# Retention attention in front of a GELU MLP: 64-token sub-chunks on four 64x64 TensorE tiles, and a new emission order

## The chip, the cores and the metric

The kernel runs on one core of a Trainium2 chip. A core has TensorE (PE, the matmul engine; its weight loads are listed apart as PEld), VectorE (DVE), ScalarE (ACT), GpSimd (POOL) and SyncE (SP), each with its own queue that it works off in order, and 16 DMA engines that all queues share. Matmuls write to PSUM, eight banks of 512 fp32 columns in each of 128 partitions; everything else lives in SBUF. The metric is the device time of one execution in microseconds.

## The reference

A retention layer (attention without softmax, with a decay per head) feeds an MLP with the exact GELU. Batch 8, 8 heads, 576 tokens, 64 per head; so 4608 tokens of 512, and 2048 hidden units.

```python
scale = 1.0 / np.sqrt(D_)
scores = scale * np.matmul(q, k.transpose(0, 1, 3, 2))
gamma = 1.0 - 2.0 ** (-5.0 - np.arange(H))
rel = pos[:, None] - pos[None, :]
Dmat = np.where(rel >= 0, gamma[:, None, None] ** rel[None, :, :], 0.0)
ret = np.matmul(scores * Dmat[None], v)          # per batch and head
x = ret.transpose(0, 2, 1, 3).reshape(B * S, H * D)
h = x @ w_in
out = (0.5 * h * (1.0 + erf(h / np.sqrt(2)))) @ w_out
```

Inputs and output are fp32; both kernels compute in bf16 with fp32 sums.

## The kernel before

**Attention in chunks.** Each sequence of 576 tokens is cut into four chunks of 128 and one of 64: 40 chunks, numbered through the batch. The decay between two tokens splits into a factor for the row and one for the column, so v is scaled once (`vh`, L242, table `dv`), the scores get only a causal mask (L235), and the output gets its factor when it leaves PSUM (L288, table `dq`). What came before a chunk enters through a running sum of k times v per head, which is kept in a PSUM bank for a whole sequence (`u_ps`, L266) and copied to SBUF by ACT after each chunk (`u_sb`, L270).

For one chunk TensorE does: transposes of q and k (`turn`, L213; 8 matmuls with an identity), which DVE or ACT copies to `qkT`; `scores` (L226: 8 matmuls, per pair of heads one on rows 0 to 63 and one on rows 64 to 127 of the array); `inner` (L260: 8 matmuls, masked scores times `vh`; L266: 4 for the running sum); and `cross` (L280: 8 matmuls, q times the running sum, on two halves of the rows). `evacuate` (L288) then writes x with tokens on partitions. The MLP wants x with features on partitions, so x is transposed once more: for chunks 0 to 8 on TensorE (`turn_x`, L302, copied at L303), from chunk 9 on by a DMA transpose from SP (L294). From chunk 9 on q and k are transposed by DMA too (L207).

**The MLP in blocks.** Nine blocks of 512 tokens. Product 1 (`mlp1_step`, L314) makes 16 tiles of 128 hidden units, four matmuls each, and ACT applies GELU (L318). Product 2 (`mlp2_step`, L343) sums 16 matmuls for each of four groups of 128 tokens; ACT copies the result (L349) and SP stores it (L350). The last group of all goes in three column pieces (L331, L334, L335).

**Order.** The scheduler is off; the kernel writes every engine's order itself. A planner keeps an estimated clock (`now`), a list of attention steps that are due (T transposes, R scores with the cross of the chunk before, S inner, U a late cross, V the scaled v, X the transpose of x), and hands out MLP steps where no attention step is due. RR takes two chunks in one visit. `LEAD`, `PAIR_LEAD` and `LATE_LEAD` limit how far attention runs ahead. Blocks 0 and 1 are cut into pieces of tokens (0 to 256, 256 to 512; 0 to 192, 192 to 320 or 448, and the rest mixed between the steps of product 2).

**PSUM.** Five banks (a to e) are shared by scores, transposes, hT and oT; two hold `o_ps`, one `u_ps`.

**Loads.** Chunk 0 comes as fp32 by three DMAs from SP (L84), which DVE casts (L132, L133). All other chunks (L137) and both weights (L149, L159; 8 pieces each) come from POOL's queue, which casts to bf16 on the way: chunks 1 to 3, w_in, chunk 4, four pieces of w_out, chunk 5, three, chunk 6, the last; then one chunk after each S.

The two lines that set how scores are spread over the array:

```python
sl = slice(64 * e, 64 * e + 64)                                    # L225
nc.tensor.matmul(sc[e][:cs, hp, :cs], lhsT=qkT[sl, 1, hp, :cs], rhs=qkT[sl, 0, hp, :cs], ...)   # L226
```

Of the kernel before, what the change touches and what calls it, by code (L numbers as in the profile page):

```python
# [13 lines left out]
ALU = mybir.AluOpType  # L14


@with_exitstack
def kernel(
# [9 lines left out]

# [8 lines left out]

    HP = H // 2
    C = 128
# [4 lines left out]
    NCH = -(-S // C)  # L48
    chunks = [(b, ci, ci * C, min(C, S - ci * C)) for b in range(B) for ci in range(NCH)]
    N_CH = len(chunks)  # L50
    N_PE_TR = 9
    N_FIRST = 4
    N_LD = 7
    LEAD = 52
    PAIR_FROM = 2
    PAIR_LEAD = 70
    LATE_LEAD = 48
# [4 lines left out]
    tr_pool = ctx.enter_context(tc.tile_pool(name="tr", bufs=9))  # L62
    ret_pool = ctx.enter_context(tc.tile_pool(name="ret", bufs=2))
    v_pool = ctx.enter_context(tc.tile_pool(name="v", bufs=5))
    x_pool = ctx.enter_context(tc.tile_pool(name="x", bufs=4))
    u_pool = ctx.enter_context(tc.tile_pool(name="u", bufs=4))
    g_pool = ctx.enter_context(tc.tile_pool(name="g", bufs=2))
    o_pool = ctx.enter_context(tc.tile_pool(name="o", bufs=4))

    PS = bass.MemoryType.PSUM  # L70

    ps = ctx.enter_context(tc.tile_pool(name="ps", bufs=1, space=PS))

    xT = const_pool.tile([128, N_DM, n_tok], BF16, name="xT")


    zeros = const_pool.tile([128, 512], BF16, name="zeros")
    nc.vector.memset(zeros, 0.0)

    clock = [0.0]  # L80
    first = []
    for nm, src in (("q32", q), ("k32", k), ("v32", v)):
        t = const_pool.tile([128, H, D], FP32, name=nm)
        nc.sync.dma_start(t, src[0, :, 0:C, :].rearrange("h s d -> s h d"))  # L84
        first.append(t)
    ident = const_pool.tile([128, 128], BF16, name="ident")
    make_identity(nc, ident)

    lg_row = const_pool.tile([128, H, 1], FP32, name="lg_row")
    for h in range(H):  # L90
        nc.vector.memset(lg_row[:, h], log_gamma[h])
    ln_scale = const_pool.tile([128, 1], FP32, name="ln_scale")
    nc.vector.memset(ln_scale, math.log(scale))
    msk = const_pool.tile([128, 1, 128], FP32, name="msk")
    nc.vector.memset(msk, 1.0)

    pos = const_pool.tile([128, 1, NCH], FP32, name="pos")
    nc.gpsimd.iota(pos[:, 0, :], pattern=[[C, NCH]], base=0, channel_multiplier=1,
                   allow_small_or_imprecise_dtypes=True)

    nc.gpsimd.affine_select(
        out=msk[:, 0, :], in_=msk[:, 0, :], compare_op=ALU.is_ge, fill=0.0, base=0,
        pattern=[[1, 128]], channel_multiplier=-1,
    )

    arg = const_pool.tile([128, H, NCH], FP32, name="arg")
    nc.vector.tensor_tensor(arg, lg_row.to_broadcast([128, H, NCH]), pos.to_broadcast([128, H, NCH]), op=ALU.mult)
    dv = const_pool.tile([128, H, NCH], FP32, name="dv")
    nc.scalar.activation(dv, arg, AF.Exp, scale=-1.0, bias=ln_scale)
    dq = const_pool.tile([128, H, NCH], FP32, name="dq")  # L110
    nc.scalar.activation(dq, arg, AF.Exp)

    warm_act = const_pool.tile([128, 1], FP32, name="warm_act")
    nc.scalar.activation(warm_act, ln_scale, AF.Gelu)


    ret_short = [const_pool.tile([128, HP, 128], BF16, name=f"ret_short{e}") for e in range(2)]
    vh_short = const_pool.tile([128, H, D], BF16, name="vh_short")
    for t in ret_short + [vh_short]:
        nc.gpsimd.memset(t, 0.0)  # L120


    loaded = {}
    land_chunk, land_in, land_out = {}, [], []
    dma_clock = [2.0]

    def load_chunk(i, now=0.0):
        b, ci, c0, cs = chunks[i]
        qk = ld_pool.tile([128, 2, H, D], BF16, tag="qk", name="qk_ld")
        if i == 0:  # L130
            v_ld = first[2]
            nc.vector.tensor_copy(qk[:, 0], first[0])  # L132
            nc.vector.tensor_copy(qk[:, 1], first[1])  # L133
        else:
            v_ld = ld_pool.tile([128, H, D], BF16, tag="v", name="v_ld")
            for dst, src in ((qk[:, 0], q), (qk[:, 1], k), (v_ld, v)):
                nc.gpsimd.dma_start(dst[:cs], src[b, :, c0:c0 + cs, :].rearrange("h s d -> s h d"))  # L137
        loaded[i] = (qk, v_ld)
        dma_clock[0] = max(dma_clock[0], now) + 3.0 * cs / C
        v_at = 6.5 if i == 0 else dma_clock[0] + (1.2 if i < N_FIRST else 1.6)  # L140
        land_chunk[i] = (v_at - 1.9, v_at - 0.9, v_at)

    W_IN_COLS = 256
    w_in_sb, w_out_sb = [], []

    def load_w_in():
        j = len(w_in_sb)
        t = const_pool.tile([128, N_DM, W_IN_COLS], BF16, name=f"w_in{j}")
        nc.gpsimd.dma_start(  # L149
            t, moe_w_in[:, j * W_IN_COLS:(j + 1) * W_IN_COLS].rearrange("(c p) f -> p c f", p=128)  # L150
        )
        w_in_sb.append(t)
        dma_clock[0] += 1.38
        land_in.append(dma_clock[0] + (1.9 if j else 1.3))

    def load_w_out():
        j = len(w_out_sb)
        t = const_pool.tile([128, 2, d_model], BF16, name=f"w_out{j}")
        nc.gpsimd.dma_start(  # L159
            t, moe_w_out[j * 256:(j + 1) * 256, :].rearrange("(c p) f -> p c f", p=128)  # L160
        )
        w_out_sb.append(t)
        dma_clock[0] += 1.38
        land_out.append(dma_clock[0] + 1.3)

    for i in range(4):
        load_chunk(i)
    for _ in range(d_ff // W_IN_COLS):
        load_w_in()
    load_chunk(4)  # L170
    for j in range(N_DF // 2):
        load_w_out()
        if j in (3, 6):
            load_chunk(5 + (j == 6))
    


    st = {i: {} for i in range(N_CH)}
    u_ps = [None]
    mlp_begun = [False]  # L180

    free_at = dict.fromkeys("abcde", 0.0)
    held = set()
    last_tag = [None]

    def first_free(n=1):
        return sorted((x for x in free_at if x not in held), key=lambda x: free_at[x])[:n]

    def bank(until, shape, dtype, name):

        tag = last_tag[0] = first_free()[0]
        free_at[tag] = clock[0] + until
        return ps.tile(shape, dtype, tag=tag, name=name)

    def tr_ps(shape, name):

        return bank(1.3, shape, BF16, name)

    def turn(i, parts=(0, 1)):

        cs = chunks[i][3]
        qk = loaded[i][0]
        if "qkT" not in st[i]:
            st[i]["qkT"] = tr_pool.tile([128, 2, HP, 128], BF16, tag="qkT", name="qkT")
        qkT = st[i]["qkT"]
        if i >= N_PE_TR:
            nc.sync.dma_start(qkT.rearrange("p j hp s -> p (j hp) s")[:, :, :cs],  # L207
                              qk[:cs].rearrange("p j h d -> p (j h d)"), transpose=True)
            return
        for j in parts:  # L210
            ps = tr_ps([128, HP, 128], "qk_ps")
            for hp in range(HP):
                nc.tensor.transpose(ps[:, hp, :cs], qk[:cs, j, 2 * hp:2 * hp + 2, :], ident[:cs, :cs])  # L213
            if i >= N_FIRST:
                nc.vector.tensor_copy(qkT[:, j, :, :cs], ps[:, :, :cs])  # L215
            else:
                nc.scalar.copy(qkT[:, j, :, :cs], ps[:, :, :cs])

    def scores(i, banks):
        cs = chunks[i][3]  # L220
        qkT = st[i]["qkT"]
        sc = [ps.tile([128, HP, 128], FP32, tag=banks[e], name=f"sc{e}") for e in range(2)]
        for hp in range(HP):
            for e in range(2):
                sl = slice(64 * e, 64 * e + 64)  # L225
                nc.tensor.matmul(sc[e][:cs, hp, :cs], lhsT=qkT[sl, 1, hp, :cs], rhs=qkT[sl, 0, hp, :cs],  # L226
                                 start=True, stop=True)
        return sc

    def masked(i, sc):  # L230
        b, ci, c0, cs = chunks[i]
        st[i]["ret"] = []
        for e in range(2):
            r = ret_short[e] if cs < C else ret_pool.tile([128, HP, 128], BF16, tag=f"ret{e}", name=f"ret{e}")
            nc.vector.tensor_tensor(r[:cs, :, :cs], sc[e][:cs, :, :cs],  # L235
                                    msk[:cs, :, :cs].to_broadcast([cs, HP, cs]), op=ALU.mult)
            st[i]["ret"].append(r)
# [8 lines left out]
    def by_parity(i):  # L246

        lo = HP * st[i]["half"]
        return st[i]["o_ps"].rearrange("p e (hp d) -> p e hp d", d=D)[:, :, lo:lo + HP]
# [357 lines left out]
```

## Time and profile before

| | |
|---|---|
| time, median of 3 runs | 312.64 us (311.79 to 312.69) |
| the profiled execution: span | 444.2 us, mean granted TensorE clock 0.658 |
| DVE busy | 101.9 us |
| ACT busy | 143.3 us |
| GELU of a 512-column tile (L318) | 0.60 us; of 256 columns 0.38, of 128 columns 0.28 |
| ACT copy of 512 columns (L349, L270) | 0.585 us |
| DVE mask of 512 columns (L235) | 0.69 us; of 256 columns 0.42 |
| DVE scaled v, 512 columns (L242) | 0.68 us |
| DMA transpose of q and k (L207), issue to landing | 5.0 us |
| DMA transpose of x (L294), issue to landing | 3.5 us |
| load of 128 tokens of q (L137), issue to landing | 5.0 us |
| first matmul of the MLP | 17.5 us after the start |
| last piece of w_out: issue, landing | 35.2 us, 8.1 us later |
| HBM read, written | 36.70 MB, 9.44 MB |

The span runs from the first to the last instruction of one execution under the profiler. It is far longer than the median of the timed runs; the profiled execution ran with TensorE throttled from about 6 us on. A group of instructions is listed by line, engine, operation and tile; "x4" is how many. Matmuls overlap in the pipeline, so the duration of one in a list is longer than the distance between two starts, which is what counts for the rate.

### The profile page before, as it was taken

The numbers are of one execution on the slowest core, as the hardware profiler recorded it, in microseconds if no ns is written. First come the engines' busy times: TensorE is split into PE (matmuls) and PEld (weight loads), VectorE is DVE, ScalarE is ACT, GpSimd is POOL, SyncE is SP. The second block draws the span as 40 slices with busy tenths as digits, with TensorE's granted clock in tenths as the row PEclk, the third lists the DMA queues.
The fourth block names the chain that finished last, engine by engine and source line by source line (L and its number), as shares of the span: only waits on it lengthen the run. The fifth ranks groups of instructions, "written<-read, shape, count | busy, mean of one in ns | idle before, by whom it ended". The sixth has DMA issues, their size and how long they took to land.

```text
span 444.2 us, 6130 instructions
## 1 busy us (share of the span) xinstructions
PE 436.6 (98%) x2522; PEld 204.9 (46%) x2522; DVE 101.9 (23%) x189; ACT 143.3 (32%) x279; POOL 112.4 (25%) x144
## 2 busy tenths in 40 slices
PE   7999999999999999999999999999999999999997
PEld 3676358855534444344433443344434333333334
DVE  4601345345332240034402500063102100000000
ACT  5664025523244213421343124311442134114411
POOL 9878524426242316004620440000000000000000
PEclk8666666666666666666666666666666666666666
DMA  9999979959999989519990991042101200010011
GB/s 136 179 189 178 127 107 144 90 62 158 159 154 72 110 105 155 60 35 167 127 161 1 121 176 47 0 84 72 41 0 49 66 25 0 24 47 26 0 46 49
DMA packets 168636, 39.40 MB, mean 89 GB/s; under 512 B 157600, under 2 KB 164128, under 8 KB 168608
## 3 DMA queue, kind: packets, MB, share of 16 engines
q0 software_dynamic: 115792, 17.97, 59.8%
q1 hardware_dynamic: 52816, 21.05, 22.5%
q8 instruction: 19, 0.31, 0.3%
q14 instruction: 9, 0.07, 0.1%
HBM read 36.70 MB, written 9.44 MB: 104 GB/s over the span
## 4 chain that ended last, share of the span: by engine, by line
PE 95%; DVE 2%; DMA 1%; POOL 1%; issue 1%; ACT 0%; DVEq 0%
PE hT L314 42%; PE oT L343 41%; PE o_ps L260 3%; PE u_ps L266 2%; PE o_ps L280 1%; PE oT L331 1%; DMA qk_ld<-in_k_dram 1%; PE qk_ps L213 1%; PE x_ps L302 0%; DVE x L288 0%; DVE vh L242 0%; DVE qkT L215 0%; POOL qk_ld L137 0%; DVE ret_966 L235 0%; DVE ret_425 L235 0%
## 5 line engine op out<-in xcount | busy, mean ns | idle before, releaser
L137 POOL DMA_DIRECT2D qk_ld<-in_q_dram x39 | 33.5, 859 | 143.7 <-PE u_ps L266 107.4
L349 ACT COPY o_sb<-oT 128x512 f32<-128x512 f32 x35 | 20.5, 585 | 138.4 <-PE oT L343 132.7
L137 POOL DMA_DIRECT2D v_ld<-in_v_dram x39 | 34.0, 872 | 1.4 <-DMA w_in_153<-in_moe_w_in_dram 0.7
L137 POOL DMA_DIRECT2D qk_ld<-in_k_dram x39 | 33.6, 861 | 0.9 <-DMA w_in_151<-in_moe_w_in_dram 0.5
L270 ACT CAST u_sb<-u_ps 128x512 bf16<-128x512 f32 x32 | 18.7, 585 | 43.9 <-PE u_ps L266 43.3
L288 DVE TENSOR_TENSOR x<-o_ps,dq 128x512 bf16<-128x512 f32 (+1 forms) x40 | 26.4, 681 | 24.5 <-PE o_ps L280 14.5
L314 PE MATMUL hT<-xT,w_in_149 128*128 128x512 bf16 (+3 forms) x96 | 25.8, 429 | 0.5 <-DMA w_in_149<-in_moe_w_in_dram 0.5
L314 PE MATMUL hT<-xT,w_in_151 128*128 128x512 bf16 (+3 forms) x96 | 26.2, 431 | 0.0
L314 PE MATMUL hT<-xT,w_in_157 128*128 128x512 bf16 (+3 forms) x96 | 26.2, 432 | 0.0
L314 PE MATMUL hT<-xT,w_in_163 128*128 128x512 bf16 (+3 forms) x96 | 26.0, 432 | 0.0
L314 PE MATMUL hT<-xT,w_in_155 128*128 128x512 bf16 (+3 forms) x96 | 26.0, 428 | 0.0
L314 PE MATMUL hT<-xT,w_in_153 128*128 128x512 bf16 (+3 forms) x96 | 25.5, 423 | 0.3 <-DVE qkT L215 0.3
L314 PE MATMUL hT<-xT,w_in_159 128*128 128x512 bf16 (+3 forms) x96 | 25.5, 427 | 0.0
L314 PE MATMUL hT<-xT,w_in_161 128*128 128x512 bf16 (+3 forms) x96 | 25.5, 428 | 0.0
L242 DVE TENSOR_TENSOR vh<-v_ld,dv 128x512 bf16<-128x512 bf16 x31 | 20.8, 678 | 0.0
L314 PEld LDWEIGHTS <-w_in_159 128*128 128x128 bf16 x96 | 10.7, 117 | 13.4 <-issue 12.2
L314 PEld LDWEIGHTS <-w_in_163 128*128 128x128 bf16 x96 | 10.9, 121 | 12.8 <-issue 12.0
L314 PEld LDWEIGHTS <-w_in_157 128*128 128x128 bf16 x96 | 11.1, 122 | 12.5 <-issue 11.5
L314 PEld LDWEIGHTS <-w_in_149 128*128 128x128 bf16 x96 | 10.8, 119 | 12.9 <-issue 11.2
L314 PEld LDWEIGHTS <-w_in_161 128*128 128x128 bf16 x96 | 10.9, 120 | 12.4 <-issue 10.9
L314 PEld LDWEIGHTS <-w_in_155 128*128 128x128 bf16 x96 | 10.9, 121 | 12.2 <-issue 11.2
L314 PEld LDWEIGHTS <-w_in_151 128*128 128x128 bf16 x96 | 11.0, 120 | 11.5 <-issue 10.6
(814 smaller groups left out, 730.3 us busy)
## 6 DMA issues: line engine op xcount, KB each, us to landing
out_dram<-o_sb SPq DMA_DIRECT2D x35, 256.0 KB, 2.4
qk_ld<-in_q_dram POOLq DMA_DIRECT2D x31, 128.0 KB, 5.0
qk_ld<-in_k_dram POOLq DMA_DIRECT2D x31, 128.0 KB, 5.3
v_ld<-in_v_dram POOLq DMA_DIRECT2D x31, 128.0 KB, 5.5
qk_ld<-in_q_dram POOLq DMA_DIRECT2D x8, 64.0 KB, 5.5
qk_ld<-in_k_dram POOLq DMA_DIRECT2D x8, 64.0 KB, 6.2
v_ld<-in_v_dram POOLq DMA_DIRECT2D x8, 64.0 KB, 5.9
qkT<-qk_ld SPq DMA_TRANSPOSE x31, 5.0
```

Of the source, the lines that this page charges most:

```text
L137: nc.gpsimd.dma_start(dst[:cs], src[b, :, c0:c0 + cs, :].rearrange("h s d -> s h d"))
L213: nc.tensor.transpose(ps[:, hp, :cs], qk[:cs, j, 2 * hp:2 * hp + 2, :], ident[:cs, :cs])
L242: nc.vector.tensor_tensor(vh[:cs], loaded[i][1][:cs], dv[:cs, :, ci:ci + 1].to_broadcast([cs, H, D]), op=ALU.mult)
L260: nc.tensor.matmul(ov[:, e, hp, :], lhsT=s["ret"][e][:, hp, :], rhs=s["vh"][:, 2 * hp + e, :], start=(hp == 0 and mate is None), stop=(ci ...
L266: nc.tensor.matmul(u_ps[0][:, hp, :], lhsT=loaded[i][0][:cs, 1, 2 * hp:2 * hp + 2, :], rhs=s["vh"][:cs, 2 * hp:2 * hp + 2, :], start=(ci = ...
L270: nc.scalar.copy(u, u_ps[0])
L280: nc.tensor.matmul(ov[:cs, e, hp, :], lhsT=s["qkT"][sl, 0, hp, :cs], rhs=s["u"][sl, hp, 64 * e:64 * e + 64], start=False, stop=(hp == HP - 1),
L288: nc.vector.tensor_tensor(x.rearrange("p hp e d -> p e hp d")[:cs], by_parity(i)[:cs], dq.rearrange("p (hp e) c -> p e hp c", e=2)[:cs, :, ...
L314: nc.tensor.matmul(hT[:, :hi - lo], lhsT=w[:, cc, o:o + 128], rhs=xT[:, cc, tok0 + lo:tok0 + hi], start=(cc == 0), stop=(cc == N_DM - 1))
L331: nc.tensor.matmul(oT[:, :hi - lo], lhsT=g_tiles[t, m][:, ts * 128:(ts + 1) * 128], rhs=w_out_sb[m // 2][:, m % 2, lo:hi], start=(m == 0), ...
L343: nc.tensor.matmul(oT, lhsT=g_tiles[t, m][:, ts * 128:(ts + 1) * 128], rhs=w_out_sb[m // 2][:, m % 2, :], start=(m == 0), stop=(m == N_DF ...
L349: nc.scalar.copy(o_sb, oT)
```

## The change

**Units of 128 tokens, sub-chunks of 64.** The tokens of all sequences are cut into 36 units of 128; a sequence of 576 is nine sub-chunks of 64, so every second sequence begins in the middle of a unit. The mask, the running sum and the cross term now work per sub-chunk.

**Four tiles.** Every attention matmul has 64 rows, 64 stationary columns and 64 moving columns. Its operands start at partition 0 or 64 and its output at partition 0 or 64, which names one of four 64x64 tiles of the array. `phase` emits two matmuls of one row half, then two of the other:

```diff
+    def p_ops(i, c):
+        s = st[i]
+        return [mm(s["px"][sl(e), c, 64 * n:64 * n + 64], lhsT=s["vh"][sl(c), HP * e + n, :],
+                   rhs=s["ret"][sl(c), n % 2, 2 * e + n // 2, :], start=True, stop=True)
+                for n in range(HP) for e in range(2)]
+    def x_ops(i, f):
+        s = st[i]
+        return [mm(s["px"][sl(p // 2), f, 256 + 128 * c + 64 * (p % 2):320 + 128 * c + 64 * (p % 2)],
+                   lhsT=(s["u"][:, 0] if c else st[i - 1]["u"][:, 1])[sl(f), p, :], rhs=s["qkT"][sl(f), 0, p, sl(c)],
+                   start=True, stop=True) for c in range(2) if not first(i, c) for p in (0, 2, 1, 3)]
+    def s_ops(i, f):
...
+    def t_ops(i, c):
...
+    def phase(top, low):
+        for n in range(0, max(len(top), len(low)), 2):
+            for op in top[n:n + 2] + low[n:n + 2]:
+                op()
```

s_ops are the scores, t_ops the new part of the running sum, p_ops scores times v, x_ops the cross term.

**Output transposed.** p_ops and x_ops put features on the partitions, so x needs no transpose. The two parts lie in different columns of `px`; ACT copies the cross part to SBUF, DVE adds and multiplies by the decay straight into xT:

```diff
-        x = s["x"] = x_pool.tile([128, HP, 2, D], BF16, tag="x", name="x")
-        nc.vector.tensor_tensor(x..., by_parity(i)[:cs], dq..., op=ALU.mult)
-        if i >= N_PE_TR:
-            nc.sync.dma_start(xT[:, :, col:col + cs], ..., transpose=True)
+        nc.scalar.copy(part[:, lo:hi]..., px[:, :, 256:]...[:, :, lo:hi])
+        nc.vector.tensor_tensor(both[:, lo:hi], own[:, lo:hi], part[:, lo:hi], op=ALU.add)
+        if len(added) == 2:
+            nc.vector.tensor_tensor(x, both, d, op=ALU.mult)
```

**Running sum in SBUF.** t_ops write only the sub-chunk's own part to PSUM; DVE adds it to an fp32 sum in SBUF (`s_run`), and ACT casts that sum to `u_sb`:

```diff
-            u = st[i + 1]["u"] = u_pool.tile([128, HP, 128], BF16, tag="u", name="u_sb")
-            nc.scalar.copy(u, u_ps[0])
+            new = s["up"][:, c, 256:]
+            if first(i, c):
+                nc.vector.tensor_copy(run[:, c], new)
+            else:
+                nc.vector.tensor_tensor(run[:, c], new, run[:, 0] if c else st[i - 1]["s"][:, 1], op=ALU.add)
+        nc.scalar.copy(u[:, lo:hi]..., run[:, lo:hi])
```

**Groups.** Units 0 to 3 run their phases S, T and X apart. From unit 4 on one group G holds p and x of unit i-1 and s and t of unit i:

```diff
+            ops = [[], []]
+            x = i - 1 if nxt["X"] == i - 1 else None
+            if x is not None:
+                new_px(x)
+                for n in range(2):
+                    ops[n] += p_ops(x, n) + x_ops(x, n)
+            if i < N_U:
+                new_st(i)
+                for n in range(2):
+                    ops[n] += s_ops(i, n) + t_ops(i, n)
+            phase(*ops)
+            if i < N_U:
+                masked(i)
+                summed(i)
+            if x is not None:
+                evacuated(x)
```

`masked` is now one DVE operation of 512 columns per unit, `summed` the DVE and ACT operations above.

**PSUM.** `st` and `px` have two banks each; hT, oT and the transposes of q and k share four (m0 to m3).

**Transposes of q and k.** On TensorE for units 0 to 5, by DMA from SP for units 6 to 35.

**Loads.** Everything comes from POOL's queue, in the order of a string (u a unit's q, k, v; i a piece of w_in; o a piece of w_out); a piece of w_in is two DMAs of 64 partitions, and a unit that spans two sequences takes six:

```diff
-    for nm, src in (("q32", q), ("k32", k), ("v32", v)):
-        nc.sync.dma_start(t, src[0, :, 0:C, :].rearrange("h s d -> s h d"))
+    for x in "uuuiiiiiuiiioouoouoouoou":
```

**Tables.** The decay of the output, now with features on partitions and tokens in columns, is built for 128 tokens and extended by DVE beside the scaled v of units 0 to 2 (`extend_dq`).

**Emission order.** The planner now estimates when DVE and ACT come free (class `Engines`) and when an hT bank does. Product 1 of a block takes whatever tokens are ready in steps of 128, and product 2 of a block starts only when product 1 of that block is complete:

```diff
+                if there > d and w <= now and bank_at() <= now:
+                    if best is None or there - d > best[3] - best[2]:
+                        best = (blk, m, d, there)
...
+            if blk == t and all(done1.get((t, m), 0) == TOK_BLK for m in range(N_DF)):
+                ts, m0, m1 = run2[t][0]
```

Block 0's product 2 goes in two pairs of token groups, two hidden tiles at a time:

```diff
-            run = [("2", t, ts, m, m + 2) for m in range(0, N_DF, 2) for ts in range(3)]
-            run += [("2", t, 3, m, m + 4) for m in range(0, N_DF, 4)]
+    run2[0] = [(ts, m, m + 2) for pair in ((0, 1), (2, 3)) for m in range(0, N_DF, 2) for ts in pair]
```

The product steps themselves and the end of the last block are as before.

## Prediction

> **What bounds the kernel now.** I read the page from the top: engines, slices, then the chain of waits.
>
> ```profile
> span 444.2 us, 6130 instructions
> PE 436.6 (98%) x2522; PEld 204.9 (46%) x2522; DVE 101.9 (23%) x189; ACT 143.3 (32%) x279; POOL 112.4 (25%) x144
> PEclk8666666666666666666666666666666666666666
> ...
> PE 95%; DVE 2%; DMA 1%; POOL 1%; issue 1%; ACT 0%; DVEq 0%
> ```
>
> TensorE is busy 98% and is 95% of the chain, but in this execution its granted clock fell within the first slice (PEclk 8, then 6; the windows below say 0.65). The chain in order of time gives the price of the pure MLP, blocks without attention beside them:
>
> ```profile
> 357.76 20.91 PE hT L314 x64
> 378.67 20.91 PE oT L343 x64
> 399.58 20.84 PE hT L314 x64
> ```
>
> 64 matmuls of 512 columns take 20.91 us, 327 ns each. All 18 such stretches would take 376 us, more than the 312.64 us median: the timed runs had a higher clock. Scaling the stretch from 16 to 441 us by 0.65 gives 276, with 16 before and 3 behind it 295 us. The missing 17.6 us are waits that do not shrink with the clock, or a clock below 1; the profile cannot say which. So every sum below is made twice: in the profile's own time (span 444.2; the page shows nothing of what lies around it) and at full clock (312.64), where an MLP matmul costs 327 x 0.65 = 214 ns. Waits that the slow matmuls cover in the profile lie open in the timed runs.
>
> The windows from one block's first hT to the next one's show what attention costs:
>
> ```profile
> 122.16:170.59 48.43, 48.43 (x277) 20.98 (x276) 14.61 (x25) 14.82 (x25) 16.89 (x20) 0.65 1.06 113
> 170.59:217.60 47.01, 47.01 (x254) 19.69 (x252) 13.95 (x24) 13.55 (x23) 13.55 (x17) 0.65 1.02 102
> 217.60:265.24 47.64, 47.64 (x262) 20.71 (x260) 9.53 (x17) 14.82 (x25) 14.63 (x18) 0.65 1.19 118
> 265.24:312.20 46.96, 46.96 (x253) 19.93 (x252) 12.54 (x22) 13.65 (x23) 0.00 (x0) 0.65 0.25 51
> 312.20:357.76 45.56, 45.56 (x221) 18.86 (x220) 4.92 (x9) 13.65 (x23) 0.00 (x0) 0.65 0.14 38
> 357.76:399.58 41.82, 41.82 (x129) 15.44 (x128) 0.00 (x0) 11.89 (x20) 0.00 (x0) 0.65 0.07 25
> ```
>
> The first number behind the window is its length, then PE, PEld, DVE, ACT, POOL. Five windows, 235.60 us, less five times 41.82, leave 26.5 us for the 24 chunks scored in them: 1.10 us per chunk, and with 40 chunks standing for 36 units 1.23 us per 128 tokens.
>
> The timeline of PE around one short chunk has the only 64x64 matmuls of this kernel:
>
> ```profile
> 110.98 0.52 PE L266 MATMUL u_ps<-vh,qk_ld 128*128 128x128 bf16 x4
> 111.43 0.21 PE L226 MATMUL sc_1628<-qkT 64*64 64x64 bf16 x1
> 111.43 0.21 PE L226 MATMUL sc_1629<-qkT 64*64 64x64 bf16 x1
> 111.48 0.19 PE L226 MATMUL sc_1628<-qkT 64*64 64x64 bf16 x1
> ...
> 111.54 0.19 PE L226 MATMUL sc_1628<-qkT 64*64 64x64 bf16 x1
> 111.55 0.19 PE L226 MATMUL sc_1629<-qkT 64*64 64x64 bf16 x1
> 111.67 0.29 PE L280 MATMUL o_ps<-u_sb,qkT 64*128 64x64 bf16 x8
> ```
>
> Two tiles start together, the next pair 0.037 us later on average, and a change of tile shape leaves a hole: 0.12 us from the last pair to L280; 0.45 us for four L266 of 0.06, so some 0.2, 0.15 of it drain.
>
> **The groups (gain).** The order of the instructions has 2176 matmuls of 64x64x64 at L240, 16 rounds of four per unit, in one visit where the old kernel makes one for scores and cross and one for inner and sums. No row shows four tiles at once. If four go as two do, a group costs 0.15 + 15 x 0.037 + 0.12 = 0.83 us in the profile's time, 0.40 below 1.23. If only two overlap, 0.15 + 31 x 0.037 + 0.12 = 1.42, 0.19 above. Four units run alone at the front, so 32 count: -12.8 or +6.1 us.
> At full clock the old chunk is cheaper too, by rows of the start: L226 at a pitch of 0.06 (6.86 to 7.04), eight L260 0.22 (12.18 to 12.40), four L266 at 0.06 0.24, eight L280 0.13 (12.85 to 12.98): 0.83; without L280, as the first of a sequence, 0.70; a short one 0.12 + 0.22 + 0.13 = 0.47; and a drain of 0.27, which two chunks of a visit share, 0.15 each. Per sequence (3 x 0.83 + 0.70 + 0.47) / 5 + 0.15 = 0.88 per chunk, 0.98 per unit. The new group lies between 0.15 + 15 x 0.03 + 0.12 = 0.72 and 0.83; I take 0.75, nearest the pitch of L260, so 0.23 x 32 = -7.4 us. Bounds: -8.3, and +7 with only two at a time (1.20).
>
> [...] In the row above the two starts of a pair are less than 0.01 us apart. [...]
>
> **Transposes (gain).** The output comes out of PSUM transposed: 36 matmuls at L302, the copies at L303 and 31 DMA transposes from SP go. Transposes of q and k fall from 72 to 48. Four cost 0.23 us (L213 pitch 0.06): 2.1 + 1.4, but those of chunks 0 to 3 lie where PE waits anyway. I take -1.5, bounds -2.4 and 0. SP's queue loses 31 issues that stood between stores and transposes of q and k; no PE wait of this trace names them, so nothing is taken.
>
> **The front (loss).** Before, DVE brings four chunks from 6.55 (vh of chunk 0) to 21.09, and ACT's last copy of x ends at 22.68; its busy time is four times 2.74 (0.68 vh, 1.37 mask, 0.69 x), so 3.5 of the 14.5 us are handovers. After, one unit needs vh 0.68, one mask 0.69, two sums of 256 (0.42 as in the 256-column mask), add 0.68 and multiply 0.68: 3.57, and the decay table 0.68 for three of them: 16.3 + 3.5. q, k, v of unit 0 leave SP and stand first in POOL: its third issue at about 3.5, landing some 4.3 later as q of chunk 1 does (3.21 to 7.52): 7.8 against 6.55. The fourth x is there at 27.6 instead of 22.7.
> Weights: w_out's last piece is issued at 35.17 and lands 8.1 later, 43.3. After, 4.5 more loads of 0.87 stand ahead of it and POOL starts 1.7 earlier: 45.5. Behind it stand 36 matmuls instead of 22 (rows 2 and 3 wait for rows 0 and 1), 3.0 us more. Block 0 so ends about 5 us later: +5, bounds +2 (only the weights, if the rest fills old waits) and +7. Splitting w_in in halves costs no DMA time: two issues of 0.69, as for the 64-row loads, match the 1.33 us in which one w_in lands.
>
> **ACT held by DVE (loss).** Before, u_sb (L270) waits for PE alone. After, ACT's copy of u waits for mask and two sums, 0.69 + 0.84 us after the group, and the Gelus stand behind it in ACT's queue; part waits there too. hT has four banks instead of a share of five. In blocks 0 and 1 the pieces are of 128 to 384 columns: four banks of 128 hold 0.86 us of PE work at full clock, of 256 1.7. So 0 to 0.9 us per group, for some eight groups; I take 0.75, since product 2 may now start only when all 16 tiles of the block are complete and cannot fill the hole: +6, bounds 0 and 7. From block 2 on, pieces of 512 columns give 3.4 us and cover it; if not, +1 us for each of 24 groups.
>
> **At nothing.** DVE's busy time rises from 102 to about 124 us, ACT's by some 20: both hide behind PE (23% and 32% busy). The tail (last product, 12 matmul chains, stores) stays.
>
> **Sums.** At full clock -7.4 - 1.5 + 5 + 6 = +2.1: 314.7 us. In the profile's own time, where slow matmuls cover ACT's wait and part of the front: 444.2 - 12.8 - 2.4 + 5 = 434.
>
> **Rivals.** (B) Faster: front and Gelu holes are hidden, since PE already waits for weights there. For: POOL's waits in the profile are w_in and w_out landings until 38 us. Against: PE has no hole over 1 us after 17 us even there, so it is late itself. -8.3 - 2.4 + 2 = 304. (C) Four tiles do not overlap, row tile by row tile only: +7 - 1.5 + 5 + 6: 329, or half of that loss 322. For: no row shows four. Against: L226's pairs leave no sign of an issue limit. It decides when a group exceeds 1.0 us.
>
> **How the numbers follow.** Forecast 0.48, its own range 312 to 318 (the terms at half their spread); B 0.40; C 0.12. About 0.3% (0.9 us) is what a measurement tells from no change: the forecast holds 0.08 within it and 0.01 below, B 0.01 within. Faster 0.40, same 0.09, slower 0.51. The range 303 to 323 reaches B's end and half of C.
>
> **What would show it.** Group time: 16 rounds at 0.03 to 0.04 us from first L240 to last. Block length at 0.65 near 45.1 (41.82 + 4 x 0.83) instead of 47 to 48. Fourth x at 27 to 28 us, block 0's last oT some 5 us late. ACT's u copy waiting for s_run, PE's hT waiting for ACT. I am wrong if PE shows no holes between 15 and 90 us at a clock near 1, or if a group takes over a microsecond.

## The result, and the profile after

The changed kernel takes 315.24 us (median of 17 runs, 312.75 to 318.36), the kernel before, beside it, 312.64 (17 runs). The ratio is 1.0074 (95%: 1.0049 to 1.0100): slower by 0.7%, some 2.3 to 2.6 us. The forecast was 314.7. The ratio compares means over the fast runs, which leaves out the two slowest of the changed kernel (318.10 and 318.36).

The profile of before that the prediction was read from had TensorE at 0.658 of its clock. The changed kernel's profile, and a second one of before taken for comparison (first experiment), run at 0.99. So the two can be set side by side. First the page of the changed kernel: span, engines, TensorE's busy tenths in 40 slices, and the shares of the chain that ended last.

```profile
span 313.5 us, 8197 instructions
PE 290.7 (93%) x3549; PEld 151.4 (48%) x3587; DVE 126.3 (40%) x259; ACT 147.8 (47%) x306; POOL 116.8 (37%) x149
PE   6769979689699999999999999999999999999995
...
PE 72%; DMA 14%; POOL 10%; issue 3%; DVE 1%; ACT 0%; POOLq 0%
```

The same lines of the kernel before, second profile:

```profile
span 311.0 us, 6094 instructions
PE 298.0 (96%) x2486; PEld 166.2 (53%) x2522; DVE 102.4 (33%) x189; ACT 142.0 (46%) x279; POOL 112.2 (36%) x144
PE   6879999899999999999999999999999999999996
...
PE 92%; DVE 3%; issue 2%; DMA 1%; POOL 1%; ACT 0%; DVEq 0%
```

TensorE is busy 7.3 us less (298.0 to 290.7) and yet the span is 2.4 us longer. Of its busy time 10.9 us after and 6.0 us before are dummy matmuls on zeros (`warm`), which the planner emits where it expects TensorE to wait, so the real work fell by some 12 us. TensorE now has holes up to the 11th slice, some 86 us, where before it had few. And the chain, 92% TensorE before, runs through DMA and POOL for a quarter of the span.

Where time is lost and won shows in windows cut at the first hT of a block (the number behind the window is its length; then PE, PEld, DVE, ACT, POOL busy, clock, DMA share, GB/s). Before: block 0, block 1, block 2, a full later block, block 7, the rest.

```profile
0.00:53.38 53.38, 46.99 (x446) 30.64 (x451) 22.57 (x52) 26.60 (x57) 43.61 (x62) 0.97 1.72 172
53.38:92.99 39.61, 38.21 (x520) 28.38 (x524) 23.81 (x43) 20.58 (x60) 21.78 (x27) 1.00 1.98 164
92.99:126.03 33.04, 32.67 (x275) 16.74 (x277) 15.13 (x25) 14.91 (x26) 16.89 (x20) 1.00 1.86 170
126.03:157.86 31.83, 31.30 (x249) 15.95 (x252) 12.26 (x21) 13.55 (x23) 10.01 (x13) 1.00 1.64 151
...
252.67:280.30 27.63, 27.47 (x127) 12.54 (x128) 0.00 (x0) 11.89 (x20) 0.00 (x0) 1.00 0.10 39
280.30:311.04 30.74, 27.76 (x159) 14.28 (x159) 0.00 (x0) 12.79 (x23) 0.00 (x0) 1.00 0.12 43
```

The same windows after:

```profile
0.00:57.89 57.89, 48.14 (x676) 29.22 (x682) 30.33 (x86) 27.05 (x69) 50.15 (x69) 0.97 1.78 160
57.89:101.11 43.22, 35.70 (x670) 22.06 (x676) 24.25 (x44) 19.68 (x51) 22.51 (x27) 1.00 2.08 148
101.11:131.49 30.38, 29.96 (x372) 14.48 (x376) 15.14 (x28) 15.01 (x29) 15.75 (x20) 1.00 1.83 165
131.49:162.03 30.54, 30.12 (x366) 14.53 (x369) 13.71 (x27) 15.04 (x28) 13.77 (x16) 1.00 1.88 163
...
253.64:282.47 28.83, 28.67 (x214) 13.26 (x216) 4.52 (x8) 12.95 (x23) 0.00 (x0) 1.00 0.10 38
282.47:313.45 30.98, 27.72 (x158) 14.32 (x159) 0.00 (x0) 12.81 (x23) 0.00 (x0) 0.99 0.12 43
```

Block 0 loses 4.5 us (57.89 against 53.38), block 1 another 3.6 (43.22 against 39.61, with 7.5 us of holes), so block 2 starts 8.1 us late. Block 2 wins 2.7 us back, each of the three full blocks after it 1.3 to 1.7. In block 7 the kernel before has no attention left (27.63, pure MLP), the changed one still has (28.83). 8.1 - 5.7 is the 2.4 us between the spans.

What the holes of block 1 wait for. The changed kernel's waits between 14 and 90 us (engine, line, what it waited for, us in total, times, longest):

```profile
ACT u_sb L330 <- DVE s_run L326: 21.6, 10, 4.3
...
DVE vh L303 <- DMA v_ld<-in_v_dram: 8.3, 4, 7.1
...
PE warm L232 <- ACT g L377: 4.4, 4, 1.8
...
PE st L240 <- DMA qkT<-qk_ld: 2.4, 1, 2.4
```

The prediction's wait is there: ACT stands at u_sb for DVE's sums, and PE stands, before its dummy matmuls, for banks that a late GELU frees (before hT itself it waits for a GELU once, 0.6 us). But DVE itself stands at vh for a late load of v, and PE at a group for a late DMA transpose. The chain of waits names the loads (start, length, what):

```profile
39.47 8.91 DMA qk_ld<-in_k_dram
...
48.91 12.53 DMA qk_ld<-in_q_dram
...
61.97 14.84 DMA v_ld<-in_v_dram
...
76.82 0.69 DVE vh L303
```

Three loads one behind the other take 8.9, 12.5 and 14.8 us from issue to landing. The medians of all DMAs issued between 40 and 90 us, before (count, size, us to landing):

```profile
qk_ld<-in_q_dram POOLq DMA_DIRECT2D x10, 128.0 KB, 6.7
qk_ld<-in_k_dram POOLq DMA_DIRECT2D x10, 128.0 KB, 7.0
v_ld<-in_v_dram POOLq DMA_DIRECT2D x9, 128.0 KB, 7.2
...
qkT<-qk_ld SPq DMA_TRANSPOSE x8, 7.6
```

And after:

```profile
qk_ld<-in_k_dram POOLq DMA_DIRECT2D x10, 128.0 KB, 11.9
v_ld<-in_v_dram POOLq DMA_DIRECT2D x10, 128.0 KB, 11.7
qk_ld<-in_q_dram POOLq DMA_DIRECT2D x10, 128.0 KB, 10.3
...
qkT<-qk_ld SPq DMA_TRANSPOSE x10, 9.3
```

The same loads take 3.6 to 4.9 us longer. The first DMA transpose is issued at 42.0 us after (unit 6) and at 54.7 us before (chunk 9).

The runs also differ in the clock that TensorE was granted. The 15 runs of the changed kernel in the ratio have 0.973 to 0.995, the runs of before beside the experiments 0.994 to 1.0. In the changed kernel's profile the lower clock is one stretch of 3.41 us at 0.50 (19.39 to 22.80 us). The six of the 15 runs with 0.993 or more take 314.4 us on average, the other nine 315.6, and before at 0.994 or 0.995 (13 runs) 312.9. At the same clock the difference is thus about 1.5 us; the rest goes with the lower clock. Why the changed kernel was granted less was not tried. The two profiles above, at 0.994 and 0.995, can be compared.

### The profile page after: what moved, and what is told of

Its sections match the earlier page's. It is cut to its first block, busy times and chain, and to the rows that moved or that the text cites. A ratio compares the mean times of both kernels' runs of the same rounds, so it can differ in the third digit from the quotient of the medians.

```text
span 313.5 us, 8197 instructions
## 1 busy us (share of the span) xinstructions
PE 290.7 (93%) x3549; PEld 151.4 (48%) x3587; DVE 126.3 (40%) x259; ACT 147.8 (47%) x306; POOL 116.8 (37%) x149
## 4 chain that ended last, share of the span: by engine, by line
PE 72%; DMA 14%; POOL 10%; issue 3%; DVE 1%; ACT 0%; POOLq 0%
PE oT L390 34%; PE hT L373 32%; DMA v_ld<-in_v_dram 5%; DMA qk_ld<-in_q_dram 4%; POOL qk_ld L116 4%; POOL w_in L127 3%; PE px L240 3%; DMA qk_ld<-in_k_dram 3%; PE st L240 2%; DMA w_out<-in_moe_w_out_dram 2%; POOL v_ld L116 2%; POOL w_out L135 1%; PE oT L406 1%; DVE s_run L326 0%; PE warm L232 0%
## 5 line engine op out<-in xcount | busy, mean ns | idle before, releaser
L373 PE MATMUL hT<-xT,w_in 128*128 128x512 bf16 (+3 forms) x708 | 131.3, 336 | 4.1 <-issue 1.8
L390 PE MATMUL oT<-w_out,g 128*128 128x512 bf16 x543 | 121.4, 379 | 2.3 <-issue 2.1
L373 PEld LDWEIGHTS <-w_in 128*128 128x128 bf16 x724 | 65.4, 98 | 59.2 <-issue 2.0
L377 ACT ACTIVATE g<-hT 128x512 bf16<-128x512 f32 (+3 forms) x181 | 84.6, 515 | 19.8 <-PE hT L373 19.0
L390 PEld LDWEIGHTS <-g 128*128 128x128 bf16 x560 | 53.6, 98 | 65.1 <-issue 2.1
L309 DVE TENSOR_TENSOR ret<-st,msk 128x512 bf16<-128x512 f32 x36 | 24.9, 691 | 79.2 <-PE st L240 79.2
L330 ACT CAST u_sb<-s_run 128x512 bf16<-128x512 f32 (+1 forms) x36 | 20.5, 570 | 63.7 <-DVE s_run L326 56.7
L347 DVE TENSOR_TENSOR both<-px,part 128x512 f32<-128x512 f32 (+1 forms) x36 | 22.8, 633 | 44.0 <-ACT part L342 44.0
L326 DVE TENSOR_TENSOR s_run<-st,s_run 128x256 f32<-128x256 f32 x49 | 20.6, 420 | 0.8
L350 DVE TENSOR_TENSOR xT<-both,dq 128x512 bf16<-128x512 f32 x28 | 19.4, 692 | 1.0
L232 PE MATMUL warm<-zeros 128*128 128x512 bf16 x26 | 10.9, 511 | 6.3 <-ACT g L377 4.4
```

The source lines that it names most:

```text
L309: nc.vector.tensor_tensor(s["ret"], s["st"][:, :, :256].rearrange("p f (hp t) -> p f hp t", hp=HP), msk.to_broadcast([128, 2, HP, HALF]), ...
L326: nc.vector.tensor_tensor(run[:, c], new, run[:, 0] if c else st[i - 1]["s"][:, 1], op=ALU.add)
L330: nc.scalar.copy(u[:, lo:hi].rearrange("p c hp d -> p c (hp d)"), run[:, lo:hi])
L347: nc.vector.tensor_tensor(both[:, lo:hi], own[:, lo:hi], part[:, lo:hi], op=ALU.add)
L350: nc.vector.tensor_tensor(x, both, d, op=ALU.mult)
L373: nc.tensor.matmul(hT[:, :hi - lo], lhsT=w[:, cc, o:o + 128], rhs=xT[:, cc, tok0 + lo:tok0 + hi], start=(cc == 0), stop=(cc == N_DM - 1))
```

## The experiments

Times are medians; the kernel before, run beside them on the same chip, stood at 312.5 each time (312.48 to 312.56). The changed kernel was not run again: differences are taken from its 315.24 us. Where the 95% interval of a run's ratio to before overlaps that of the changed kernel (1.0049 to 1.0100), the difference is not clear of the noise, and the text says so.

**The kernel before again, for a profile.**

> The kernel before, unchanged, for a profile at another clock than 0.658, so that its stages can be set beside those of the changed kernel (span 313.5 us at 0.994). Theory (the prediction): a full block of before lasts about 27.7 + 4.4 x 0.88 = 31.6 us at full clock, so the changed kernel's 30.5 us is 1.1 us better per block and about 7 us over the middle; block 0 of before ends about 5 us earlier than that of the changed kernel, and before loses some 6 us less in its blocks 0 and 1. Rival: before's own start is no earlier; then the two kernels differ by less than 3 us at the end of block 1 and the groups bring nothing.

312.74 us, span 311.0, clock 0.995. The rival fell: block 0 ends 4.5 us earlier and block 1 8.1 us earlier in before. A full block takes 31.83 to 32.17 us, not 31.6, so the changed kernel wins 1.4 us per block rather than 1.1.

**Only two tiles at a time.**

```diff
-            for op in top[n:n + 2] + low[n:n + 2]:
-                op()
+        for op in top + low:
+            op()
```

> The changed kernel with each group's matmuls in another order: all of the upper row half first, then all of the lower (the same 64 instructions, the same order everywhere else), so that only two of the four tiles can be at work at once. Theory (the prediction's group term): matmuls of different row halves overlap, so a group of 64 costs 0.15 + 31 x 0.037 + 0.12 = 1.4 us against 0.72 measured from block to block; 32 groups: +14 us or more against the changed kernel, where PE has no holes to hide it (some 25 groups: +17). Rival: four tiles do not overlap more than two, the pitch is that of the instruction stream; then the time is the same within 2 us.

324.86 us (ratio to before 1.041, 1.036 to 1.046): +9.6 against the changed kernel. Its full blocks:

```profile
133.80:165.72 31.92, 31.50 (x365) 15.91 (x368) 13.66 (x26) 15.03 (x28) 11.61 (x14) 1.00 1.72 151
165.72:197.65 31.93, 31.51 (x366) 15.93 (x369) 13.10 (x26) 15.03 (x28) 12.01 (x15) 1.00 1.13 115
```

31.92 against 30.54: 0.35 us for each of four groups, so a group costs 1.08 instead of 0.73. The theory holds, its 14 us were almost half too many. And 31.92 is what before needs (31.94 on average): without the overlap of the row halves the new groups win nothing in a block.

**The u_sb copy on DVE, in the old order.**

```diff
-        nc.scalar.copy(u[:, lo:hi]..., run[:, lo:hi])
+        nc.vector.tensor_copy(u[:, lo:hi]..., run[:, lo:hi])
```

> The changed kernel with the copy of the running sum to bf16 (u_sb) on DVE instead of ACT, everything else in the same order. ACT's queue then never waits for DVE's sums. Theory (the prediction: ACT held by DVE costs 0.75 us for each of 8 groups): 4 to 6 us faster than the changed kernel. Rival: the holes of 58 to 85 us come from late loads and transposes (the profile's chain runs through loads of k, q and v of 9 to 15 us there); then within 1.5 us of the changed kernel.

313.86 us, -1.4: the rival's number, and not clear of the noise (ratio 1.0014 to 1.0090). ACT's wait for s_run is gone, but most of the holes are not. Block 1 still takes 43.28 us, with 5.1 us of holes instead of 7.5; this profile has 6.8 us at a clock of 0.50 there (60.5 to 63.9 and 77.6 to 81.0 us), so its block lengths do not give the gain. In place of ACT's wait, between 38 and 90 us:

```profile
DVE vh L303 <- DMA v_ld<-in_v_dram: 17.0, 5, 6.8
```

DVE waits for v twice as long as in the changed kernel, with the mask and sums of a finished group queued behind. One wait had covered part of the other.

**Units 6 to 8 transposed by TensorE.**

```diff
-    N_PE_TR = 6
+    N_PE_TR = 9
```

> The changed kernel with q and k of units 6, 7 and 8 transposed by TensorE (24 more matmuls, some 1.4 us) instead of by DMA, as the kernel before does for its first nine chunks; the planner lays out the order anew. Theory (late loads and transposes make the holes of block 1): the DMA transposes from 42 to 61 us go, groups 6 to 8 no longer wait for them, and the loads behind land earlier; 3 to 6 us faster. Rival (ACT held by DVE): 1 to 2 us slower by the added matmuls.

313.24 us, -2.0 with 24 matmuls more on TensorE (ratio 0.9992 to 1.0066, which still overlaps). Neither number: better than the rival allowed, less than the theory asked.

**The u_sb copy on DVE, known to the planner.** The first edit again, and its time in the planner's clock.

```diff
-        s["at"]["u"] = eng.run("ACT", eng.free["DVE"], 0.58)
+        s["at"]["u"] = eng.run("DVE", now, 0.43)
```

> The changed kernel with the u_sb copy on DVE, as in the run before with the same edit, but now the planner knows it, so that the order is laid out anew (its own sum of planned gaps falls from 22 to 13 us). Theory (ACT's queue, with Gelus behind copies, also sets the planned holes of blocks 0 and 1): 4 to 8 us faster than the changed kernel, under 311 us. Rival (late loads of v and late DMA transposes set these holes): no better than the copy on DVE in the old order, 313 to 315 us, with DVE standing at vh for v_ld.

312.61 us, -2.6 (0.9979 to 1.0025, clear of the changed kernel): just under the rival's range, 1.6 us short of the theory's. In its profile DVE still waits 12.2 us for v_ld between 10 and 90 us.

**Both edits.**

> Both edits in one kernel, the planner knowing both: u_sb copied by DVE, and units 6 to 8 transposed by TensorE. If ACT's waits and the late loads are two costs in series, the gains add up or more (1.4 + 2.0 us or more: 311.5 us or less). If one covers the other, it is no better than the better of the two, 313 us.

308.06 us (0.9834, 0.9793 to 0.9874): -7.2, more than 2.6 + 2.0. Its blocks 0 and 1:

```profile
0.00:57.47 57.47, 47.12 (x782) 30.57 (x789) 39.01 (x105) 25.58 (x71) 50.63 (x70) 1.00 1.73 158
57.47:93.31 35.84, 32.65 (x563) 17.59 (x568) 24.04 (x48) 16.08 (x34) 21.69 (x27) 1.00 2.06 156
```

Block 1 ends at 93.3 us, where before's ends at 93.0: all of the 8.1 us are back, though block 0 is still 4.1 us longer than before's, and what is left is the gain from block 2 on. The costs are in series, and each hides part of the other's cure: the ACT copy costs 1.4 to 2.6 us while loads are late and 5.2 once they are not (313.24 to 308.06); the DMA transposes cost 2.0 while ACT is held and 4.6 once it is not (312.61 to 308.06). In all but the 1.4 the planner also laid out another order, and no run takes that apart.

**vh emitted later.**

```diff
-            got.append((land[i][2], "V", i))
+            got.append((land[i][2] + 4.0, "V", i))
```

> The changed kernel with the u_sb copy on DVE in the old order, and with vh of each unit emitted 4 us later by the planner's clock, since the trace showed DVE standing at vh for a late v_ld for 17 us (5 times) between 38 and 90 us with mask and sums queued behind it. Theory (the head of DVE's queue holds the mask of a group that is ready): 2 to 4 us faster than without the shift (313.9 us). Rival (the group itself needs those loads): within 1 us of it, since the wait only moves.

314.06 us against 313.86: nothing in sum. But the shift holds back vh of the first units too: the fourth x comes at 34.45 us instead of 31.66 and block 0 ends 1.5 us later, while block 1 is 2.3 us shorter (40.96 against 43.28, where the other profile had its 6.8 us at half clock). So a gain in block 1 of about the size of the loss in block 0 is not excluded. That the group itself needs those loads fits, but is not shown.

**Unit 0 from SP.**

```diff
+        nc.sync.dma_start(t, src[0, :, 0:U, :].rearrange("h s d -> s h d"))
...
+        nc.vector.tensor_copy(loaded[0][0][:, j], first32[j])
```

> The changed kernel with unit 0 loaded as fp32 by three DMAs from SP and cast by DVE, as the kernel before does; POOL's queue starts with unit 1. Theory (the prediction's front term: loads ahead of the weights and of the fourth unit cost block 0 about 5 us): everything behind on POOL's queue is 2.6 us earlier, 2 to 3 us faster than the changed kernel. Rival (block 0 is set by ACT's queue, where the copies of the cross part stand behind Gelus): within 1 us of the changed kernel.

317.13 us, 1.9 slower (1.0072 to 1.0168, which overlaps the changed kernel's): the theory missed, and the rival by 0.9. The loads did come earlier (vh of unit 3 runs at 21.57 us instead of 25.65), but the planner laid out another order, with unit 1's transposes ahead of unit 0's output, and the fourth x came at 32.69 us instead of 31.74. The run says only that earlier loads do not by themselves bring the fourth x.

**Units 9 to 11 by TensorE too.** In the 308.06 us kernel:

```diff
-    N_PE_TR = 9
+    N_PE_TR = 12
```

> The 308.06 us kernel (u_sb copied by DVE, units 6 to 8 transposed by TensorE) with units 9 to 11 transposed by TensorE too: 24 more matmuls, some 1.4 us. Theory (DMA transposes in block 1 hold up the loads: from the first of them on, a load takes 9 to 17 us from issue to landing instead of 5 to 8): another 1 to 3 us faster, 305 to 307 us. Rival (only units 6 to 8 were late, since their transposes stood on the path of the groups themselves): 1 to 2 us slower, 309 to 310 us.

306.28 us (0.9811, 0.9772 to 0.9851): another 1.8 us, as the theory said, and the lowest median of the study; with four runs each the two intervals still overlap. TensorE is busy 14.84 and 14.51 us of the 15 us slices at 60 and 75 us, where the changed kernel has 12.35 and 11.72.

**The DMA transposes back, without a reader.** In the 308.06 us kernel, behind TensorE's transposes:

```diff
+        if j == 1 and 6 <= i < 9:
...
+            nc.sync.dma_start(spare..., qk..., transpose=True)
```

> The 308.06 us kernel with the DMA transposes of units 6, 7 and 8 added again, into spare tiles that nobody reads; the groups take TensorE's transposes as before. Theory (contention: the DMA transposes slow the loads behind them): it gives back most of the 4.5 us that TensorE's transposes had brought, 311 to 312.5 us. Rival (the groups waited for the landing of their own DMA transpose, some 9 us, and the loads did not matter): 308 to 309 us.

313.76 us: 5.7 us lost, all that the step had won and 1.1 more. The medians of DMAs issued from 40 to 90 us, first in the 308.06 us kernel:

```profile
v_ld<-in_v_dram POOLq DMA_DIRECT2D x11, 128.0 KB, 8.1
...
qkT<-qk_ld SPq DMA_TRANSPOSE x8, 8.9
```

and with the three spare transposes:

```profile
v_ld<-in_v_dram POOLq DMA_DIRECT2D x10, 128.0 KB, 11.7
...
qkT<-qk_ld SPq DMA_TRANSPOSE x7, 8.8
spare<-qk_ld SPq DMA_TRANSPOSE x3, 9.0
```

Nobody waits for the spare tiles, TensorE, DVE, ACT and POOL work in the same order as in the 308.06 us kernel, and yet loads from another queue take 11.7 us again instead of 8.1. They lengthen with the first transpose. In the 308.06 us kernel it is issued at 56.0 us, and the loads issued from 42 to 56 us have a median of 7.8 us, those from 56 to 66 us 14.0; here the first is issued at 43.5 us, and the medians are 12.2 and 13.4. So here the DMA transposes cost by what they do to the loads (11.7 us instead of 8.1), at least where the groups do not wait for them. What in the DMA engines is shared was not tried; the spare transposes also stand ahead of units 9 to 11 in SP's queue (unit 9's is issued at 60.0 us instead of 56.0) and hold a load buffer longer, and no run took these apart.

**w_out first.** In the 308.06 us kernel (u: a unit, i: a piece of w_in, o: of w_out):

```diff
-    for x in "uuuiiiiiuiiioouoouoouoou":
+    for x in "uuuiiiiiuiiiooooouoouou":
```

> The 308.06 us kernel with five pieces of w_out ahead of unit 4 in POOL's queue instead of two, and units 4 to 7 behind. Theory (the front term: the last w_out sets the end of block 0, where PE waits 2.3 us for w_out): w_out lands some 2.5 us earlier, 1 to 2 us faster, 306 to 307 us. Rival (block 1 needs the units as much as block 0 needs the weights): within 1 us or slower.

309.79 us, 1.7 slower (0.9885 to 0.9937, clear of the 308.06 us kernel's). In this kernel the wait for w_out is real, though TensorE's part of it is 1.4 us (the 2.3 of the expectation take in 0.9 of POOL's): TensorE is busy 14.85 us of the slice from 45 to 60 us instead of 13.41. But the slices at 60 and 75 us fall from 14.02 and 12.95 to 13.80 and 12.60: what block 0 wins (1.7 us), block 1 loses (2.5 us). Why is not shown. Units 4 to 6 are issued 1.7 to 3.1 us later, but from unit 8 on within 0.5 us or earlier (their loads of v); the new string also has one u less, so unit 7 comes with the later loads (0.8 us later); and the profile has 3.4 us at half clock there (84.1 to 87.5 us).

**The same part of the change in the kernel before.** Likewise where the planner asks for it; x as before.

```diff
+    N_QK_TR = 6
...
-        if i >= N_PE_TR:
+        if i >= N_QK_TR:
             nc.sync.dma_start(qkT..., qk..., transpose=True)
```

> The kernel before with one part of the change alone: q and k of chunks 6, 7 and 8 by DMA transposes instead of by TensorE (N 9 to 6, x as before); its planner lays out the order anew. Theory (early DMA transposes are what costs block 1, in either kernel): loads issued from 40 us on take 10 us or more to land instead of 7, and the time rises by 3 to 6 us to 315 to 318 us, like the 4.5 us between the two kernels with the u_sb copy on DVE. Rival (the old order, with product 2 mixed into block 1, covers it): within 1 us of 312.5 us.

321.93 us (1.031, 1.024 to 1.038): +9.4, beyond the theory's range. Loads issued from 40 to 90 us take 8.4, 9.7 and 10.2 us (q, k, v) instead of 6.7, 7.0 and 7.2. Its chain has links that before has not:

```profile
49.48 5.55 DMA v_ld<-in_v_dram
55.03 10.99 DMA qkT<-qk_ld
66.07 0.61 PE sc L227 x7
...
79.87 10.05 DMA qkT<-qk_ld
89.98 0.44 PE sc L227 x8
```

Here TensorE's scores wait for the landing of the transposes themselves too (2.2 us in four waits between 30 and 110 us). That its planner laid out a new order, and 6.8 us at half clock (from 63.5 and from 101.1 us), are part of the difference.

## Why the prediction was right in sum, and where it was wrong

**Clock.** Right: the sum at full clock was the one to use. A pure MLP block takes 27.63 us, 216 ns a matmul (predicted 214). The other sum, 434 us in the profile's own time, stays untested: no run of the changed kernel was granted a clock of 0.65.

**Groups.** Right mechanism, off in size. Old unit: (31.94 - 27.63) / 4 = 1.08 us against 0.98; new group (30.54 - 27.63) / 4 = 0.73 against 0.75; gain 0.35 instead of 0.23. But it was to count 32 times, and in blocks 0 and 1 TensorE was waiting anyway. From block 2 on all gains together are 5.7 us, not 8.9. One group of a full block in the timeline (start, us, what):

```profile
142.62 0.32 PE L240 MATMUL px<-ret,vh 64*64 64x64 bf16 x16
142.77 0.30 PE L240 MATMUL px<-qkT,u_sb 64*64 64x64 bf16 x16
142.90 0.30 PE L240 MATMUL st<-qkT 64*64 64x64 bf16 x16
143.02 0.31 PE L240 MATMUL st<-vh,qk_ld 64*64 64x64 bf16 x16
143.26 0.39 PE L373 MATMUL hT<-xT,w_in 128*128 128x512 bf16 x1
```

Sixteen matmuls, four rounds, start every 0.13 us: 0.033 per round, inside the 0.03 to 0.04 that was to be seen. That is 8 ns per matmul.

From the first to the last of the 64 the rows show about 0.5 us, and the length of a full block leaves 0.73 for a whole group.

**Transposes.** This step failed. It took 60 matmuls fewer on TensorE (2.1 + 1.4 us) as a gain of 1.5 us and let the work vanish. The output's 36 do vanish; the 24 of units 6 to 8 move to DMA, 12.6 us earlier than before's first, into the stretch where units and stores are on the way too. That costs 2.0 us net alone, 4.6 without the ACT wait. The prediction took nothing for SP's queue because it loses 31 issues; it looked at the queue's count and not at when its first transposes fall. The column to look at stood in the prediction's own windows: a DMA share of 1.02 to 1.19 in every block that still has loads, of 0.07 to 0.25 in the others.

**Front.** +5 predicted, +4.5 measured (57.89 against 53.38): the number was right, the path was not. The last w_out landed when it was predicted to (issued at 37.9 us, 7.6 us later, 45.5), but no TensorE instruction of the changed kernel waits for w_out. Between product 1 and product 2 of block 0 stands:

```profile
40.22 0.38 PE L390 MATMUL oT<-w_out,g 128*128 128x512 bf16 x1
42.38 1.24 PE L232 MATMUL warm<-zeros 128*128 128x512 bf16 x5 [1.79 <-ACT g L377]
43.68 9.23 PE L390 MATMUL oT<-w_out,g 128*128 128x512 bf16 x42
```

TensorE waits 1.8 us for a bank that a GELU frees, and runs product 2 from 43.68 to 57.89 us with hardly a hole. With 36 matmuls behind a landing at 45.5 us (36 x 0.216) and one group (0.73) the block would have ended near 54 us, an estimate. So block 0 lost its time to the fourth x, which came at 31.74 us instead of 27.6, and to ACT, whose cost the prediction had as a term of its own. What sets the fourth x stays open: in the runs above with the u_sb copy on DVE, units 6 to 8 by TensorE, both, or unit 0 from SP it came between 31.57 and 32.69 us, in the one with vh emitted later at 34.45.

**ACT held by DVE.** +6 predicted. The wait is there (21.6 us at u_sb), and taking it away is worth 1.4 us alone (within the noise), 2.6 with the order laid out for it, 5.2 where loads are in time. The sign that was named, hT waiting for ACT, shows for 0.6 us alone; another 4.4 stand before the dummy matmuls. Block 1's loss of 3.6 us is this and the late loads together. From block 2 on it is covered, as said: 30.54 us per block with 0.4 of holes.

**At nothing.** DVE 126 (predicted 124). ACT rose by 6, not 20, since its Gelus fell from 93.3 to 84.6 us in fewer pieces (192 to 181). Both hidden.

**Rivals.** Faster (B) fell, TensorE's holes up to 86 us are there. Four tiles that do not overlap (C) fell. The sum, +2.1 against +2.4 between the spans, came out by errors that cancel, which is luck: the gains were 5.7 us and not 8.9, the losses of blocks 0 and 1 were 8.1 and not 11, the late loads in block 1 were not on the list, and neither was the lower clock. Two slips had no consequence: half of C's loss gives 321 us, not 322, and the scores of short chunks are not the only 64x64 matmuls of before (64 of L280 are so too).

## What to carry to other kernels

Work taken off TensorE to DMA is not gone (here the transposes of units 6 to 8, 1.4 us of TensorE's time by estimate, cost 2.0 us net, 4.6 without the ACT wait): ask when the transfer falls and which loads it stands among. Two waits in series hide each other, so an edit that cures one may show a fraction of its worth (here 1.4 or 2.6 us alone, 5.2 beside the other cure); cure both before judging either. A gain per unit counts only for units that run where that engine is the bound, here from block 2 on.

## What the runs showed of the hardware

In the changed kernel, matmuls on four 64x64 tiles start 8 ns apart on average, 64 of them in about 0.5 us; with one row half after the other the same 64 cost 0.35 us more.

With three added DMA transposes and the same order on the computing engines, loads of v on another queue took 11.7 us instead of 8.1 (medians of those issued from 40 to 90 us). In the 308.06 us kernel a transpose of q and k lands 8.9 us after its issue, a load of v 8.1.
